# Set-up of a recurrent attention kernel: first score product in quarters between weight products, paired transposes, and dummy matmuls in idle gaps

## Chip, core and metric

The kernel runs on one core of one Trainium2 chip. The metric is device time in microseconds (us). The kernel before had a median of 1601.96 us in its first three timed runs.

## The reference, cut to what matters

```python
def _A_ref(x, mem0, Wq, Wk, Wv, Wo, seg_len):        # 64 segments of 32 rows, 8 memory rows
    for s in range(n_seg):                            # strictly one after the other
        h = concatenate([mem, xs], axis=1)            # 40 rows x 448
        q, k, v = h @ Wq, h @ Wk, h @ Wv              # 16 heads of 256
        p = softmax(where(mask, q @ k.T * scale, -1e9))
        o = (p @ v) @ Wo
        mem = o[:, :8]                                # feeds the next segment
def _B_ref(x, W_gate, W_up, W_down): ...              # gated feed-forward, 448 -> 1792 -> 448
x = x + A(layernorm(x)); x = x + B(layernorm(x)); x = x + A(layernorm(x)); x = x + B(layernorm(x))
```

The kernel multiplies the weights together first. For each head, M = Wk Wq^T gives scores as h M h^T, and B = Wv Wo gives outputs as p (h B). These products are the set-up. Then 70 steps follow, one segment of each of two layers at a time.

## The kernel before

The set-up loads Wk and Wq transposed by DMA (`load_kq`), and Wv and Wo plain (`load_vo`). `make_M(i)` makes M for four heads, and `make_B(j)` makes B for two heads, after transposing Wv on TensorE.

```python
def make_B(j):
    wn, wo = vo.pop(j)
    wv = bp.tile([P, 4, DM], BF, tag="wv", name="wv")
    for a in range(2):                       # 16 transposes through PSUM
        ...
        copy_out(wv[:, 2 * a:2 * a + 2, :], tp[:, :, 0:DM])
    for hh in range(2):
        for mt in range(3):                  # 16 matmuls of 448 columns, with the tails
            ...
    ...
load_vo(0); load_vo(1); load_kq(0)
make_B(0); load_vo(2); make_B(1); load_vo(3); load_kq(1); make_M(0)
...                                          # mem0, layernorm of the first two x tiles
for j in (2, 3): make_B(j); load_vo(j + 2)
load_kq(2); make_M(1); load_kq(3)
for j in (4, 5): make_B(j); load_vo(j + 2)
in_order(nc.sync.dma_start(x_ring[:, 2:R, :], ...))
make_M(2); make_M(3)
for g in range(nsteps):
    ...
    if g == 0:
        def mid(): make_B(6)                 # between the first G and the scores
        def soft(): make_B(7); late_pools()  # after the softmax was started
    ...
    step(g, inG, mid, soft, before, late, end, last)
    ...
fill(1, 20)                                  # the last feed-forward
```

Each step begins with G = M h, 224 matmuls with 40 or 80 moving columns into PSUM (`gps`). Scores (`S_ps`), softmax, values (`vps`), the transposes of P (`PT_ps`), the weighted sum (`AT_ps`) and the new memory (`mps`) follow. `tails` are the products of the last 64 of the 448 rows. They read `MT_sb`, and the full ones read `M_sb`.

```python
        def tail(self, i):
            t, half = self.t0 + i, HALVES[self.side]
            self.mm(t, MT_sb[half, t * 128:(t + 1) * 128], hT[half, 3, c0:c1, :])
        ...
        first = [pair_of_banks(k) for k in range(nA)]
        tails(first)
        for pr in first:
            for bk in pr:
                bk.full()
                bk.out()
```

In the profiles PE is TensorE, DVE VectorE, ACT ScalarE, POOL GpSimd and SP SyncE, whose queue issues the loads. In the timelines below its pieces of work run in the order of the program: while it waits in front of one (1.28 us for wq before M3), nothing from behind it runs.

## Time and profile before

| | kernel before |
|---|---|
| three timed runs | 1601.85 to 1602.24 us |
| the profiled execution | 1604.42 us (its span 1602.6) |
| M3 starts | 56.12 us |
| first G starts | 61.63 us |
| G of step 1 starts | 90.62 us |
| last matmul of M3 (61.35) to G of step 1 | 29.27 us |

The profiled execution was 2.5 us longer than the median of the timed runs.

The page of the kernel before, its line of busy times and its chain of work that ended last:

```profile
PE 1564.1 (98%) x38808; PEld 1177.5 (73%) x38808; DVE 941.8 (59%) x2154; ACT 659.4 (41%) x1502; POOL 143.0 (9%) x370
...
PE 92%; DVE 4%; SPq 2%; DMA 2%; ACT 1%; issue 0%; POOL 0%; POOLq 0%; ACTq 0%
```

TensorE bounds the kernel: PE is busy for 98% of the span and makes up 92% of the chain. For this change the question is only where PE stands still, and for that the timeline is the right view.

The timeline of PE in the kernel before, from M3 to G of step 1. Columns are start, duration, line, operation, shape and count. The bracket gives the idle time before, and what ended it.

```profile
56.12 5.58 PE L126 MATMUL ps<-wq,wk 128*128 128x448 bf16 x32 [1.28 <-DMA wq<-in_A_Wq_dram]
61.63 0.57 PE L126 MATMUL gps<-hTr,MT_sb 64*128 64x40 bf16 x32
62.13 2.99 PE L126 MATMUL gps<-hTr,M_sb 128*128 128x40 bf16 x112
66.60 2.00 PE L126 MATMUL gps<-hTr,M_sb 128*128 128x40 bf16 x56 [1.48 <-issue]
...
71.36 2.95 PE L126 MATMUL ps<-wo,wv 128*128 128x448 bf16 x16 [0.61 <-ACT wv L187]
...
77.72 2.95 PE L126 MATMUL ps<-wo,wv 128*128 128x448 bf16 x16 [1.23 <-DVE wv L189]
...
81.96 0.36 PE L126 MATMUL vps<-BT_sb,memTp 64*32 64x448 bf16 x2 [0.80 <-DVE BT_sb L189]
...
90.62 0.57 PE L126 MATMUL gps<-hTr,MT_sb 64*128 64x40 bf16 x32 [0.28 <-DVE hTr L631]
```

Read it as a list of holes: 1.28 for the load of wq, 1.48 that no semaphore explains ("issue"), 0.61 and 1.23 for copies of transposed Wv, 0.80 for a copy of B. In the second half of the first G the matmuls also run slower: 56 take 2.00 us, while 112 took 2.99 us before. The table by stretches shows a granted clock of 0.50 there. Its columns are the stretch, its length, the busy time of PE, PEld (weight loads), DVE, ACT and POOL, then PEclk, the granted clock (1.00 is full), the DMA share and GB/s:

```profile
66.00:68.00 2.00, 1.40 (x43) 1.40 (x43) 0.00 (x0) 0.00 (x0) 0.00 (x0) 0.68 0.03 8
68.00:70.00 2.00, 2.00 (x52) 1.67 (x49) 0.66 (x1) 0.56 (x1) 0.00 (x0) 0.50 0.00 0
```

The sync queue issues loads without a break from 0.7 to 58 us. These are its last four transposed issues, with start and duration:

```profile
34.79 7.04 SPq L165 DMA_TRANSPOSE wk<-in_A_Wk_dram  x1
41.88 4.51 SPq L165 DMA_TRANSPOSE wq<-in_A_Wq_dram  x1
46.49 3.46 SPq L165 DMA_TRANSPOSE wk<-in_A_Wk_dram  x1
50.00 3.88 SPq L165 DMA_TRANSPOSE wq<-in_A_Wq_dram  x1
```

### The profile page before, as it was taken

How to read it: one execution, taken by the hardware profiler on the slowest of the kernel's cores; microseconds unless marked ns; L12 is line 12 of the kernel's file. 1: busy time of each engine (PE TensorE's matmuls, PEld its weight loads, DVE VectorE, ACT ScalarE, POOL GpSimd, SP SyncE). 2: the span in 40 equal slices, each digit the busy share in tenths (PEclk: the TensorE clock that was granted, in tenths of full speed). 3: DMA queues.
4: the chain of work that ended last, by engine and by line, in shares of the span. 5: the costliest groups of instructions: out<-in, count | busy, mean ns of one | idle time of the engine just before them, and what ended most of it. 6: DMA issues, size and time to landing. Idle time of an engine off the chain costs nothing.

```text
span 1602.6 us, 82607 instructions
## 1 busy us (share of the span) xinstructions
PE 1564.1 (98%) x38808; PEld 1177.5 (73%) x38808; DVE 941.8 (59%) x2154; ACT 659.4 (41%) x1502; POOL 143.0 (9%) x370
## 2 busy tenths in 40 slices
PE   7889999999999999999999999999999999999998
PEld 4467677777777777877778777877778777877675
DVE  6545556656656566656655566556655556556554
ACT  5533344434444344434444344434344343434333
POOL 2000001000101001000100101000100101000000
PEclk9999999999999999999999999999999999999999
DMA  9631000000000000000000000000000000000000
GB/s 238 148 96 34 5 6 4 6 11 6 5 10 6 11 6 10 6 11 6 5 11 6 11 6 10 6 11 6 5 11 6 8 5 6 6 8 6 7 5 9
DMA packets 49541, 31.22 MB, mean 19 GB/s; under 512 B 31656, under 2 KB 48304, under 8 KB 49200
## 3 DMA queue, kind: packets, MB, share of 16 engines
q1 hardware_dynamic: 49168, 25.93, 6.5%
q8 instruction: 303, 4.96, 1.2%
q14 instruction: 38, 0.31, 0.1%
q10 hardware_dynamic: 32, 0.01, 0.0%
HBM read 14.00 MB, written 1.84 MB: 10 GB/s over the span
## 4 chain that ended last, share of the span: by engine, by line
PE 92%; DVE 4%; SPq 2%; DMA 2%; ACT 1%; issue 0%; POOL 0%; POOLq 0%; ACTq 0%
PE gps L126 30%; PE vps L126 28%; PE gate L126 11%; PE AT_ps L126 7%; PE S_ps L126 6%; PE dps L126 5%; PE PT_ps L129 2%; DMA wq<-in_A_Wq_dram 2%; SPq L165 1%; PE tps L129 1%; DVE vox L382 1%; PE up L126 1%; PE ps L126 1%; PE mps L126 1%; DVE ssum L534 0%
## 5 line engine op out<-in xcount | busy, mean ns | idle before, releaser
L126 PE MATMUL gps<-hTr,M_sb 128*128 128x80 bf16 (+1 forms) x11760 | 417.7, 198 | 1.6 <-issue 1.5
L126 PEld LDWEIGHTS <-M_sb 128*128 128x128 bf16 x11760 | 406.2, 99 | 5.9 <-issue 1.8
L460 DVE CAST G<-gps 128x480 bf16<-128x480 f32 (+3 forms) x326 | 193.9, 612 | 237.3 <-PE gps L126 237.1
L126 PEld LDWEIGHTS <-hTr 128*32 128x32 bf16 (+3 forms) x7936 | 197.0, 96 | 145.2 <-issue 38.7
L460 ACT CAST G<-gps 128x480 bf16<-128x480 f32 (+3 forms) x326 | 165.7, 527 | 325.2 <-PE gps L126 325.2
L126 PE MATMUL vps<-B_sb,hTr 128*32 128x448 bf16 x4608 | 241.9, 353 | 0.0
L126 PE MATMUL gate<-xnT,Wgu 64*128 64x128 bf16 x3136 | 202.7, 216 | 1.0 <-ACT xnT L305 1.0
L126 PE MATMUL up<-xnT,Wgu 64*128 64x128 bf16 x3136 | 203.2, 216 | 0.0
L126 PEld LDWEIGHTS <-Wgu 64*128 64x128 bf16 x6272 | 181.4, 94 | 19.2 <-issue 12.4
L382 ACT CAST VOm<-vps 128x448 bf16<-128x448 f32 x245 | 118.9, 529 | 144.8 <-PE vps L126 144.6
L126 PE MATMUL vps<-B_sb,memTp 128*32 128x448 bf16 x3360 | 171.7, 353 | 0.0
L382 ACT CAST vox<-vps 128x448 bf16<-128x448 f32 x192 | 99.4, 533 | 159.3 <-PE vps L126 159.3
L126 PEld LDWEIGHTS <-memTp 128*32 128x32 bf16 (+1 forms) x4480 | 98.5, 94 | 82.1 <-issue 3.7
L382 DVE CAST vox<-vps 128x448 bf16<-128x448 f32 x192 | 116.5, 619 | 58.9 <-PE vps L126 58.8
L318 DVE SCALAR_TENSOR_TENSOR hh<-gate,ut 128x256 bf16<-128x256 f32 x224 | 94.7, 423 | 66.3 <-ACT ut L317 66.2
L126 PEld LDWEIGHTS <-PT 128*64 128x64 bf16 x2048 | 96.4, 110 | 39.4 <-issue 18.9
L317 ACT CAST ut<-up 128x256 bf16<-128x256 f32 x224 | 83.8, 374 | 63.1 <-PE up L126 61.9
L126 PE MATMUL AT_ps<-VOm,PT 128*64 128x320 bf16 (+1 forms) x1280 | 97.7, 261 | 1.2 <-DVE PT L576 1.2
L528 DVE TENSOR_REDUCE mx<-S_ps 104x8 f32<-104x320 f32 (+1 forms) x140 | 62.2, 486 | 59.2 <-PE S_ps L126 59.2
L126 PE MATMUL gps<-hTr,MT_sb 64*128 64x80 bf16 (+1 forms) x3920 | 91.3, 195 | 2.7 <-ACT hTr L631 1.6
L126 PE MATMUL dps<-Wd,hh 128*128 128x448 bf16 x448 | 92.6, 353 | 0.0
L126 PE MATMUL S_ps<-G,hTr 128*40 128x160 bf16 (+1 forms) x1792 | 88.1, 245 | 0.7
(89 smaller groups left out, 1428.0 us busy)
## 6 DMA issues: line engine op xcount, KB each, us to landing
wo<-in_A_Wo_dram SPq DMA_DIRECT2D x8, 448.0 KB, 5.3
wvn<-in_A_Wv_dram SPq DMA_DIRECT2D x8, 384.0 KB, 3.7
y<-mb SPq DMA_DIRECT2D x96, 28.0 KB, 1.8
out_dram<-x_ring SPq DMA_DIRECT2D x16, 112.0 KB, 1.7
Wgu<-in_B_W_gate_dram SPq DMA_DIRECT2D x7, 224.0 KB, 3.3
Wgu<-in_B_W_up_dram SPq DMA_DIRECT2D x7, 224.0 KB, 3.5
Wd<-in_B_W_down_dram SPq DMA_DIRECT2D x7, 224.0 KB, 3.3
x_ring<-in_A_x_dram SPq DMA_DIRECT2D x10, 112.0 KB, 2.0
```

Source lines behind the costliest of these rows:

```text
L126: in_order(nc.tensor.matmul(*a, **k))
L129: in_order(nc.tensor.transpose(*a))
L165: in_order(nc.sync.dma_start_transpose(t[:], srcs[n][:, 1024 * i:1024 * (i + 1)]))
L317: recent["ut"] = nc.scalar.copy(ut[:], gu[1][:])
L318: recent["hh"] = nc.vector.scalar_tensor_tensor(out=self.hh[:, f:f + 2, :], in0=gu[0][:], scalar=0.0, in1=ut[:], op0=ALU.max, op1=ALU.mult)
L382: op = self.evac[2 * x + e](self.dst[:, 2 * e + x, :], self.ps[x][e][:, 0:DM])
L460: op = (cp_a, cp_v)[self.side](G[:, self.side, self.t0:self.t0 + self.n, c0:c1, :], self.ps[:, 0:self.n * NP].rearrange("p (m c t) -> p m ...
L528: nc.vector.tensor_reduce(mx[RR, e], S3, axis=AX.X, op=ALU.max)
```

## The change

The intent is to move PE work out of the serial stretch after the last load into the waits for loads, to hide copies behind other work, and to keep PE busy in short idle gaps. The diff, cut to its core (the class `Bank` only moves, and `GPhase.run` is the old code):

```diff
+    def turn_B(j):                      # the transposes, taken out of make_B
...
+        def quarter(self, k):
+            pr = self.pair((7, 7, 7, 7), k)
+            self.tails(pr)
+            for bk in pr:
+                bk.full()
+                bk.out()
...
+    def make_two(j):
+        turn_B(j)
+        turn_B(j + 1)
+        for i in (j, j + 1):
+            make_B(i)
+            load_vo(i + 2)
+
+    def warm(n):
+        ps = psum.tile([P, 512], F32, tag="ps", name="warm")
+        for _ in range(n):
+            matmul(ps[:, 0:DM], ident[:], M_sb[:, 0, 0:DM], start=True, stop=True)
...
+    first_G.append(GPhase(0))
+    first_G[0].quarter(0)
     make_M(1)
     load_kq(3)
-    for j in (4, 5):
-        make_B(j)
-        load_vo(j + 2)
+    make_two(4)
...
+    first_G[0].quarter(1)
     make_M(2)
+    first_G[0].quarter(2)
     make_M(3)
+    turn_B(6)
+    turn_B(7)
+    first_G[0].quarter(3)
...
             def mid():
                 make_B(6)
+                make_B(7)
             def soft():
-                make_B(7)
                 late_pools()
...
+        if g in (1, 3):
+            def before():
+                warm(5)
...
+    warm(10)
     fill(1, 20)
```

More of the change, by code (lines that the diff above doesn't have):

```diff
@@ L215, in make_M @@
             store_M(MT_sb[:, 896 * i:896 * i + 896], e, ps[:, 0:DM])
-    def make_B(j):
-        wn, wo = vo.pop(j)
-        wv = bp.tile([P, 4, DM], BF, tag="wv", name="wv")
+    wv_T = {}
+    def turn_B(j):
+        wn = vo[j][0]
+        wv = wv_T[j] = bp.tile([P, 4, DM], BF, tag="wv", name="wv")
         for a in range(2):
@@ L227, in make_B @@
             copy_out(wv[:, 2 * a:2 * a + 2, :], tp[:, :, 0:DM])
+    def make_B(j):
+        wv, wo = wv_T.pop(j), vo.pop(j)[1]
         for hh in range(2):
@@ L420, in build_kernel, with __init__, mm, full @@
     cp_v = nc.vector.tensor_copy
+    class Bank:
+        def __init__(self, gp, side, t0, n):
+            self.gp, self.side, self.t0, self.n = gp, side, t0, n
+            self.ps = psum.tile([P, 512], F32, tag="ps", name="gps")
+            self.fresh = True
+        def mm(self, t, w, rhs):
+            o = (t - self.t0) * self.gp.NP
+            matmul(self.ps[:, o:o + self.gp.NP], w, rhs, start=self.fresh, stop=False, skip_group_check=True)
+            self.fresh = False
+        def full(self):
+            gp = self.gp
+            for t in range(self.t0, self.t0 + self.n):
+                m = 7 * (2 * (t // 7) + self.side) + t % 7
+                for kd in range(3):
+                    self.mm(t, M_sb[:, kd, m * 128:(m + 1) * 128], gp.hT[:, kd, gp.c0:gp.c1, :])
+        def tail(self, i):
+            gp = self.gp
+            t, half = self.t0 + i, HALVES[self.side]
+            self.mm(t, MT_sb[half, t * 128:(t + 1) * 128], gp.hT[half, 3, gp.c0:gp.c1, :])
+        def out(self):
+            gp = self.gp
+            op = (cp_a, cp_v)[self.side](
+                gp.G[:, self.side, self.t0:self.t0 + self.n, gp.c0:gp.c1, :],
+                self.ps[:, 0:self.n * gp.NP].rearrange("p (m c t) -> p m c t", m=self.n, t=L))
+            if self.side:
+                load_when(op)
+                recent["G"] = op
+                if not self.t0:
+                    recent["G1"] = op
@@ new lines, in build_kernel, with __init__, pair, tails @@
+    class GPhase:
+        def __init__(self, g):
+            chains = [c for c in (C1, C2) if 0 <= g - c.lag < nseg]
+            self.both = len(chains) == 2
+            self.c0, self.c1 = chains[0].cid, chains[-1].cid + 1
+            self.NP = L * (self.c1 - self.c0)
+            self.hT = hTr[:, g % NR]
+            self.G = p_vo.tile([P, 2, NGH, 2, L], BF, tag="G", name="G")
+        def pair(self, banks, k):
+            return [Bank(self, side, sum(banks[:k]), banks[k]) for side in range(2)]
+        @staticmethod
+        def tails(pr):
+            for i in range(pr[0].n):
+                for bk in pr:
+                    bk.tail(i)
+        def quarter(self, k):
+            pr = self.pair((7, 7, 7, 7), k)
+            self.tails(pr)
+            for bk in pr:
+                bk.full()
+                bk.out()
+        def run(self, inG):
+            banks = (6, 6, 6, 6, 4) if self.both else (7, 9, 12)
+            nA = 3 if self.both else 2
+            first = [self.pair(banks, k) for k in range(nA)]
+            for pr in first:
+                self.tails(pr)
+            for pr in first:
+                for bk in pr:
+                    bk.full()
+                    bk.out()
+            inG()
+            then = [self.pair(banks, k) for k in range(nA, len(banks))]
+            for pr in then:
+                for bk in pr:
+                    bk.full()
+            for pr in then:
+                self.tails(pr)
+                for bk in pr:
+                    bk.out()
@@ L422, in step @@
+    first_G = []
     def step(g, inG, mid, soft, before, late, end, last):
@@ L431, in step @@
         hT = hTr[:, rg]
-        G = p_vo.tile([P, 2, NGH, 2, L], BF, tag="G", name="G")
-        banks = (6, 6, 6, 6, 4) if both else (7, 9, 12)
-        class Bank:
-            def __init__(self, side, t0, n):
-                self.side, self.t0, self.n = side, t0, n
-                self.ps = psum.tile([P, 512], F32, tag="ps", name="gps")
-                self.fresh = True
-            def mm(self, t, w, rhs):
-                o = (t - self.t0) * NP
-                matmul(self.ps[:, o:o + NP], w, rhs, start=self.fresh, stop=False, skip_group_check=True)
-                self.fresh = False
-            def full(self):
-                for t in range(self.t0, self.t0 + self.n):
-                    m = 7 * (2 * (t // 7) + self.side) + t % 7
-                    for kd in range(3):
-                        self.mm(t, M_sb[:, kd, m * 128:(m + 1) * 128], hT[:, kd, c0:c1, :])
-            def tail(self, i):
-                t, half = self.t0 + i, HALVES[self.side]
-                self.mm(t, MT_sb[half, t * 128:(t + 1) * 128], hT[half, 3, c0:c1, :])
-            def out(self):
-                op = (cp_a, cp_v)[self.side](
-                    G[:, self.side, self.t0:self.t0 + self.n, c0:c1, :],
-                    self.ps[:, 0:self.n * NP].rearrange("p (m c t) -> p m c t", m=self.n, t=L))
-                if self.side:
-                    load_when(op)
-                    recent["G"] = op
-                    if not self.t0:
-                        recent["G1"] = op
@@ L469, in pair_of_banks @@
-        def pair_of_banks(k):
-            t0 = sum(banks[:k])
-            return [Bank(side, t0, banks[k]) for side in range(2)]
-        def tails(pairs):
-            for pr in pairs:
-                for i in range(pr[0].n):
-                    for bk in pr:
-                        bk.tail(i)
-        nA = 3 if both else 2
-        first = [pair_of_banks(k) for k in range(nA)]
-        tails(first)
-        for pr in first:
-            for bk in pr:
-                bk.full()
-                bk.out()
@@ L486, in step @@
-        inG()
-        then = [pair_of_banks(k) for k in range(nA, len(banks))]
-        for pr in then:
-            for bk in pr:
-                bk.full()
-        for pr in then:
-            tails([pr])
-            for bk in pr:
-                bk.out()
+        gp = first_G[0] if g == 0 else GPhase(g)
+        if g:
+            gp.run(inG)
+        G = gp.G
         S_ps = [psum.tile([P, 512], F32, tag="ps", name="S_ps") for _ in HALVES]
@@ L673, in build_kernel @@
     load_kq(0)
-    make_B(0)
-    load_vo(2)
-    make_B(1)
-    load_vo(3)
+    make_two(0)
     load_kq(1)
@@ L686, in build_kernel @@
         prep_pe(C1, t)
-    for j in (2, 3):
-        make_B(j)
-        load_vo(j + 2)
+    make_two(2)
     load_kq(2)
+    first_G.append(GPhase(0))
+    first_G[0].quarter(0)
     make_M(1)
     load_kq(3)
-    for j in (4, 5):
-        make_B(j)
-        load_vo(j + 2)
+    make_two(4)
     if R > 2:
         in_order(nc.sync.dma_start(x_ring[:, 2:R, :], x_dram[256:R * 128].rearrange("(t p) d -> p t d", p=P)))
+    first_G[0].quarter(1)
     make_M(2)
+    first_G[0].quarter(2)
     make_M(3)
+    turn_B(6)
+    turn_B(7)
+    first_G[0].quarter(3)
     nc.gpsimd.tensor_copy(memTp[0][:, :, 0:16], hTr[:, 1, :, 0, 0:16])
```

## The prediction

> **What bounds the kernel.** TensorE: on the page PE is busy 98% of the span and the chain that ended last is 92% PE. From 240 to 1440 us the table by stretches shows PE 99.3 to 99.8% busy at granted clock 1.00. The change touches none of that: in instruction order only set-up, step 0 and three places for dummy matmuls differ, and the DMA order is identical. Only the first 90 us and the last 15 can move.
>
> **Set-up (0 to 62 us).** The sync queue issues without a break from 0.7 to 58 us and DMA is saturated (share 1.03 to 1.16 from 10 to 60 us). The weight products M0 to M3 each wait for their transposed wq: idle 0.33, 0.88, 1.59, 1.28 us, starting at 17.45, 33.31, 49.26, 56.12. Those arrivals stay. PE also waits 0.3 to 1.2 us per weight transpose for its copy-out (wv, 3.9 us in all).
> **After the last load (61.6 to 90.6 us).** Everything is serial on PE: the whole first G (61.63 to 69.3), with a 1.48 us stall called "issue" and the clock at 0.50 until about 70; two make_B with their transposes (to 80.6; waits 0.61 and 1.23), softmax entangled with their copies, 0.8 us wait for BT_sb, P transposes at 86.28, step 1's G at 90.62.
> [...]
>
> **What the change does.**
> 1. G(0) becomes four quarters, three of them moved between M products, into DMA waits. A quarter is about 1.33 us (5.33 us for the same work in step 1). Off the tail: 4 us, the stall (1.5) and most of the half-clock loss (about 1.5).
> 2. Transposes are paired, so copy-outs hide: 0.61+1.23 us in step 0, and set-up slack that absorbs quarters 0 and 1.
> 3. make_B(6), (7) both precede softmax: the waits for BT_sb and Px vanish.
> Cost: quarter 2 sits directly behind M2 and needs M2's last MT_sb copy, which ended 0.85 us after M2 (55.69 against 54.84). So M3 starts about 57.0: +0.9.
> Estimated schedule: M3 ends 62.6; transposes to 64.75; quarter 3 to 66.1; mask 66.35; B6, B7 to 72.1; scores 73.3; values and P transposes at 77.9 instead of 86.28. Gain 8.4 us.
> 4. warm(5) in steps 1 and 3: 448-column matmuls at 0.189 us each, 0.94 us inside an idle of 1.12: 0 to +0.1. The clock was already 1.00.
> 5. warm(10) before the last feed-forward: 1.89 us into an idle of 1.15, at clock 1.00: the tps transposes move from 1589.20 to 1589.77: +0.57.
>
> Net -7.8 us: predicted **1594.3 us**, range 1592.6 to 1597.0. Chances: faster by over 2% 0.005; within 2% 0.985; slower 0.01.
>
> **What would show it.** Right: M0 to M2 start within 0.5 us of before; M3 near 57.0, behind quarter 2 and its copy; no "issue" stall and clock 1.00 from 62 to 72; no wait for wv in step 0; P transposes of step 0 near 78, step 1's G near 82.2; steady part as long as before; tps about 0.6 later relative to the last score step. Wrong: M3 still at 56.1; a stall or half clock elsewhere.
>
> **What would make it wrong.** [...] half clock returning in step 0 (+2); the last wvn landing after 63; quarter 2 waiting less (-0.9); warm(5) delaying the P transposes; the clock in the last feed-forward being lower in unprofiled runs, so that warm(10) gains.

-8.4 us up to the P transposes of step 0 and +0.57 for `warm(10)` come to the -7.8. The 0.189 us of a 448-column matmul is in the trace: in `dps` of the kernel before (1585.23 us) the matmuls start 0.189 to 0.199 us apart.

## The result, and the profile after

| | before | after |
|---|---|---|
| median of timed runs, these rounds | 1602.46 us (12 runs, 1600.36 to 1604.98) | 1596.06 us (10 runs, 1594.58 to 1598.37) |
| ratio, 95% interval | | 0.996 (0.9951 to 0.997) |
| M3 starts | 56.12 us | 57.10 us |
| G of step 1 starts | 90.62 us | 83.65 us |
| last matmul of M3 to G of step 1 | 29.27 us | 19.66 us |

Ratios here and below are the mean time of one kernel's fast runs over that of the other's in the same rounds, so they are not quite the ratio of the medians quoted.

The page of the changed kernel, the same two lines:

```profile
PE 1567.5 (98%) x38828; PEld 1179.3 (74%) x38828; DVE 941.9 (59%) x2155; ACT 659.2 (41%) x1503; POOL 142.9 (9%) x370
...
PE 93%; DVE 3%; DMA 2%; SPq 1%; ACT 0%; issue 0%; POOL 0%; ACTq 0%
```

The timeline of PE in the changed kernel, from M2 to G of step 1:

```profile
48.48 5.58 PE L126 MATMUL ps<-wq,wk 128*128 128x448 bf16 x32 [0.34 <-DMA wq<-in_A_Wq_dram]
54.32 0.24 PE L126 MATMUL gps<-hTr,MT_sb 64*128 64x40 bf16 x6 [0.26 <-ACT MT_sb L187]
54.97 0.27 PE L126 MATMUL gps<-hTr,MT_sb 64*128 64x40 bf16 x8 [0.41 <-ACT MT_sb L187]
55.17 1.22 PE L126 MATMUL gps<-hTr,M_sb 128*128 128x40 bf16 x42
57.10 7.25 PE L126 MATMUL ps<-wq,wk 128*128 128x448 bf16 x32 [0.70 <-DMA wq<-in_A_Wq_dram]
64.28 1.96 PE L129 MATMUL tp<-ident,wvn 128*128 128x128 bf16 x32
66.17 0.34 PE L126 MATMUL gps<-hTr,MT_sb 64*128 64x40 bf16 x14
66.45 1.23 PE L126 MATMUL gps<-hTr,M_sb 128*128 128x40 bf16 x42
...
67.85 5.83 PE L126 MATMUL ps<-wo,wv 128*128 128x448 bf16 x32
...
83.65 0.57 PE L126 MATMUL gps<-hTr,MT_sb 64*128 64x40 bf16 x32 [0.28 <-DVE hTr L664]
```

From the end of M3 to the scores no hole is left: the waits of 1.48, 0.61, 1.23 and 0.80 us are gone. Two things are new. M3 takes 7.25 us where it took 5.58, and it starts 0.98 us later, again after a wait for wq. The table by stretches shows the half clock again, now inside M3:

```profile
57.00:58.00 1.00, 0.90 (x3) 0.40 (x3) 0.00 (x0) 0.00 (x0) 0.00 (x0) 0.55 0.90 263
58.00:59.00 1.00, 1.00 (x5) 0.38 (x3) 0.62 (x1) 0.21 (x1) 0.00 (x0) 0.50 0.83 125
```

The last four transposed issues of the changed kernel:

```profile
34.96 7.49 SPq L165 DMA_TRANSPOSE wk<-in_A_Wk_dram  x1
42.49 3.59 SPq L165 DMA_TRANSPOSE wq<-in_A_Wq_dram  x1
46.18 4.86 SPq L165 DMA_TRANSPOSE wk<-in_A_Wk_dram  x1
51.09 3.85 SPq L165 DMA_TRANSPOSE wq<-in_A_Wq_dram  x1
```

The first of the four is long in both. Of the other three, now the third of the list is long, where the second was.

At the end of the span, the kernel before and then the changed kernel: the last half of a feed-forward (`dps`), and the first transposes of the last one (`tps`):

```profile
1585.23 2.82 PE L126 MATMUL dps<-Wd,hh 128*128 128x448 bf16 x14
1589.20 0.56 PE L129 MATMUL tps<-ident,xd 128*128 128x128 bf16 x7 [1.15 <-DVE xd L263]
```

```profile
1578.45 2.82 PE L126 MATMUL dps<-Wd,hh 128*128 128x448 bf16 x14
1581.11 2.06 PE L126 MATMUL warm<-M_sb,ident 128*128 128x448 bf16 x10
1583.00 0.55 PE L129 MATMUL tps<-ident,xd 128*128 128x128 bf16 x7
```

From the start of `dps` to `tps` is 3.97 us before and 4.55 us after. The ten dummies do not fit their gap and cost 0.58 us.

### The profile page after: what moved, and what is told of

Its sections match the earlier page's. It is cut to its first block, busy times and chain, and to the rows that moved or that the text cites. A ratio compares the mean times of both kernels' runs of the same rounds, so it can differ in the third digit from the quotient of the medians.

```text
span 1596.4 us, 82645 instructions
## 1 busy us (share of the span) xinstructions
PE 1567.5 (98%) x38828; PEld 1179.3 (74%) x38828; DVE 941.9 (59%) x2155; ACT 659.2 (41%) x1503; POOL 142.9 (9%) x370
## 3 DMA queue, kind: packets, MB, share of 16 engines
q8 instruction: 303, 4.96, 1.2%
## 4 chain that ended last, share of the span: by engine, by line
PE 93%; DVE 3%; DMA 2%; SPq 1%; ACT 0%; issue 0%; POOL 0%; ACTq 0%
PE gps L126 30%; PE vps L126 28%; PE gate L126 11%; PE AT_ps L126 7%; PE S_ps L126 6%; PE dps L126 6%; PE PT_ps L129 2%; PE ps L126 2%; PE tps L129 1%; DVE vox L388 1%; DMA wq<-in_A_Wq_dram 1%; SPq L165 1%; PE up L126 1%; PE mps L126 1%; DMA wvn<-in_A_Wv_dram 0%
## 5 line engine op out<-in xcount | busy, mean ns | idle before, releaser
L455 DVE CAST G<-gps 128x480 bf16<-128x480 f32 (+2 forms) x327 | 193.9, 610 | 232.9 <-PE gps L126 232.5
L455 ACT CAST G<-gps 128x480 bf16<-128x480 f32 (+2 forms) x327 | 165.8, 525 | 321.8 <-PE gps L126 321.8
```

The costliest lines, as they stand in the source:

```text
L455: op = (cp_a, cp_v)[self.side](gp.G[:, self.side, self.t0:self.t0 + self.n, gp.c0:gp.c1, :], self.ps[:, 0:self.n * gp.NP].rearrange("p (m ...
```

## The experiments

Twelve runs were made, three of them of an unmodified kernel, and all gave correct results. Timed intervals are about 2 us wide either way, so most verdicts rest on one profile of each kernel. These measures are used:

- the *tail*: from the start of the last matmul of M3 to the start of G of step 1;
- a *half-clock window*: a record of granted clock 0.5. Every such window inside a kernel, once the clock was full, lasted 3.413 us;
- the listed clock of each execution: 1.000, 0.999, 0.998 and 0.997 are read as 0, 1, 2 and 3 such windows (one window is 3.413/2 of 1600 us, so 0.1%). In all fourteen profiles this agrees with the windows counted inside the kernel.

### 1. Two more looks at the changed kernel

No edit. The control ran once with the second batch (`after_again`) and once with the last (`after_third`).

> The changed kernel unmodified, as the control of this batch and for a second profile. In the ten runs so far seven had a mean clock of 1.000 and three 0.999, and the three were about 2.2 us longer. Theory: the half-clock window that the first profile shows inside M3 (57.1 to 60.5 us) comes and goes between executions, so runs fall in two groups about 2 us apart that the listed clock separates; a profile that catches none has M3 at 5.6 us instead of 7.25 and step 1's G start 8.4 to 8.7 us before that of the kernel before (90.62). Rival: the half clock is there always and the groups are something else; then M3 takes 7.25 us in this profile too.

> The changed kernel unmodified, as control on the same chip as the repaired one. Expected: 5 to 7 us below the kernel before; last tps about 0.58 us later after step 69's start than in profiles without the ten dummies; M3 7.7 to 8.7 us after M2.

| | time, median | ratio to before | M3 start | M3 to the transposes behind it | tail |
|---|---|---|---|---|---|
| first profile | 1596.06 | 0.996 | 57.10 | 7.18 | 19.66 |
| after_again | 1596.78 | 0.9968 (0.9954 to 0.9982) | 56.59 | 5.52 | 19.69 |
| after_third | 1598.70 | 0.9965 (0.9952 to 0.9978) | 57.74 | 7.09 | 19.66 |

The tail is the same to 0.03 us. The half-clock window inside M3 comes and goes: it was there in the first and third profile (57.1 and 57.6 us), and not in the second, where M3 took 5.58 us:

```profile
56.59 5.58 PE L126 MATMUL ps<-wq,wk 128*128 128x448 bf16 x32
```

So a part of the spread between executions is the clock, as expected. It is not all of it: in `after_again` the two executions with a window were 4 us longer than the three without, and not 2.2. Two expected sizes were missed: in `after_again` G of step 1 started 9.1 us before that of the kernel before (8.4 to 8.7 expected), and in `after_third` M3 started 9.06 us after M2 (7.7 to 8.7 expected).

### 2. The kernel before

> The kernel before, unmodified, for a second profile. Theory [...]: the stall inside the first G of step 0 is there again, 0.5 to 2 us, and the third 16 KiB instruction packet of the span starts [...]after 62 us. Rival (an accident of one execution): no idle over 0.3 us inside the first G. The number and place of half-clock windows may differ from the first profile (66.7 us).

Its single time was 1606.06 us. There was no stall at all in the first G: 168 full products in one row, and a tail of 26.60 us where the first profile had 29.27. This contradicts the expectation that the stall is always there. The timeline of PE:

```profile
63.14 0.57 PE L126 MATMUL gps<-hTr,MT_sb 64*128 64x40 bf16 x32
63.64 4.40 PE L126 MATMUL gps<-hTr,M_sb 128*128 128x40 bf16 x168
```

The records tie the stall to an instruction packet that starts late. The DMA records of the trace give the start of each 16 KiB packet of the instruction queue (q8: 303 packets, 4.96 MB), and the instruction records give how many PE instructions, weight loads included, had started by then:

| profile with a whole first G behind M3 | third packet starts | PE instructions started by then | stall |
|---|---|---|---|
| before | 64.20 us | 901 | 1.48 us, after instruction 961 |
| before_warm5 (below) | 65.33 us | 839 | 0.55 us, after instruction 961 |
| before_again | 64.07 us | 771 | none |
| before_x_late (below) | 62.01 us | 771 | none |

Both stalls stand behind the same instruction, and they end 2.40 and 2.25 us after the packet's start. In the two profiles without a stall, the next instruction started 2.40 and 2.43 us after the packet. So in all four it started 2.25 to 2.43 us after the packet did, and PE stood still where the packet was late. That PE waits there for the packet is the reading of these four profiles. The packet's start differs between executions (62.01 to 65.33 us). The rival, that the burst of small matmuls stalls by itself, is out: the burst is the same in all four. The cause supposed, that full DMA engines hold the packet back, was a guess and is not shown: from 63 to 64 us, just before the packet's start, the DMA share was 0.23 in the kernel before, with the stall, and 1.02 in `before_again`, without one.

### 3. The kernel before with the large x load moved away

```diff
-    in_order(nc.sync.dma_start(x_ring[:, 2:R, :], ...))
...
             def mid():
+                loads.append((x_ring[:, 2:R, :], ...))   # issued at the softmax of step 0
                 make_B(6)
```

> The kernel before with the 448 KB load of x tiles 2 to 5 issued at the softmax of step 0 instead of at 57.5 us, so that the DMA queues are empty some 1.5 us earlier. Nothing in PE's order changes. Theory [...]: the stall in the first G shrinks to under 0.7 us, and step 1's G starts 1 to 3 us earlier. Rival (the stall comes from the burst of 144 pairs of small instructions itself): it stays at about 1.5 us.

No stall, a tail of 26.61 us, and the third packet at 62.01 us. The time did not fall: 1604.09 us, ratio 1.0003 (0.999 to 1.0015). The profile had a half-clock window in step 1 (99.3 us), which cost 1.37 us there. Since `before_again` had no stall either, one profile cannot show that the move removed it. The third packet did start earlier than in the other three (64.07 to 65.33 us), but that the load delays it is not shown.

### 4. Each main part of the change alone

`only_quarters` keeps the four quarters, and undoes the pairing, the order and the dummies. `no_quarters` keeps the pairing and the order. Both edits are shortened, and comments stand for the rest:

```diff
 # only_quarters
     def make_two(j):
-        turn_B(j)
-        turn_B(j + 1)
         for i in (j, j + 1):
+            turn_B(i)
             make_B(i)
...
 # make_B(7) and its transposes back in soft(), no warm(5), no warm(10)

 # no_quarters
-        gp = first_G[0] if g == 0 else GPhase(g)
-        if g:
-            gp.run(inG)
+        gp = GPhase(g)
+        gp.run(inG)         # the whole G at the start of step 0, after turn_B(6), turn_B(7)
 # the four calls of quarter() and first_G.append() taken out
 # no warm(5), no warm(10)
```

> Of the change only step 1: G(0) in four quarters; transposes not paired, make_B(7) back behind the score matmuls, no dummy matmuls. If the quarters carry most of the gain as the forecast had it (4 us of G, 1.5 of stall, 1.5 of half clock, less 0.9), the time is 4.5 to 6.5 us below the kernel before, and 2 to 3.5 us above the changed kernel. If pairing and order carry most, it is less than 3 us below the kernel before. No stall of the kind called issue is expected in step 0[...].

> Of the change only the paired transposes and both make_B before the softmax; the first G is whole, in step 0, after the transposes of tiles 6 and 7; no dummy matmuls. Forecast's accounting: 3.8 to 5.3 us below the kernel before, and about 3 us above the changed kernel. [...]

| | ratio to before | tail | gain in the tail against the undisturbed 26.60 |
|---|---|---|---|
| quarters alone | 0.9987 (0.9975 to 1.0) | 23.73 | 2.87 us |
| pairing and order alone | 0.9979 (0.9967 to 0.9991) | 23.47 | 3.13 us |
| the whole change | 0.996, 0.9968, 0.9965 | 19.66 to 19.69 | 6.9 us |

The quarters gained about 2.1 us in time (0.13% of 1602; 0 to 4.0 by the interval), and not the expected 4.5 to 6.5; their median lay 5.1 us above the changed kernel, where 2 to 3.5 were expected. That accounting took a stall of 1.5 us and a half clock as given. Of three profiles of this order one had both, one a stall of 0.55 us alone, and one neither. Pairing and order gained 3.4 us (1.4 to 5.3), a little below what was expected (3.8 to 5.3), but not clear of it. In `no_quarters` the equally long first G ran without a stall (the third packet started at the 712th instruction), which says no more than `before_again` does.

The two parts together gain 0.9 us more in the tail than separately. The timeline of `only_quarters` shows why: without the transposes in between, quarter 3 stands directly behind M3 and waits for its copy, which the paired transposes hide in the whole change.

```profile
57.87 5.58 PE L126 MATMUL ps<-wq,wk 128*128 128x448 bf16 x32
63.92 0.64 PE L126 MATMUL gps<-hTr,MT_sb 64*128 64x40 bf16 x14 [0.47 <-DVE MT_sb L189]
```

### 5. The dummies in steps 1 and 3

`no_warm5` is the changed kernel without them, and `before_warm5` is the kernel before with them.

```diff
 # no_warm5
-        if g in (1, 3):
-            def before():
-                warm(5)
 # before_warm5: the same three lines added to the kernel before
```

> The changed kernel without the five dummy matmuls in steps 1 and 3. Theory (idle filler): no change in time, steps 1 and 3 both 14.69 us as before. Rival (they guard the clock): some executions get a half-clock window in step 1 or 3, with a listed clock of 0.999 or 0.998 and about 1.7 us more, so the mean rises by 0.3 to 1.7 us.

> The kernel before with only the five dummy matmuls in steps 1 and 3. Theory (idle of 1.65 us in one 3.4 us window lets the clock fall in step 1 or 3 in some executions, and each such window costs 1.4 us there): the listed clock loses fewer windows than the kernel before, whose nine runs of the last batch lost 1.6 windows on average (1.000, 0.999, 0.998, 0.997 read as 0, 1, 2, 3), and the time falls by 0.5 to 1.5 us. Rival, which the forecast held (clock there is full anyway): no change in clock or time.

The timeline of PE in `no_warm5`, step 1. The row with `AT_ps` takes 3.20 us, where the same row takes 1.72 us in the changed kernel:

```profile
92.48 0.27 PE L129 MATMUL PT_ps<-ident,Px 40*128 40x40 bf16 x4 [1.12 <-DVE Px L575]
92.95 0.27 PE L129 MATMUL PT_ps<-ident,Pm 40*128 40x40 bf16 x4 [0.20 <-DVE Pm L575]
93.55 3.20 PE L126 MATMUL AT_ps<-VOm,PT 128*64 128x320 bf16 x16 [0.33 <-DVE PT L609]
```

The table by stretches of `no_warm5` puts the half clock there:

```profile
92.00:94.00 2.00, 0.98 (x10) 0.68 (x11) 1.13 (x3) 0.71 (x2) 0.00 (x0) 0.87 0.73 229
94.00:96.00 2.00, 2.00 (x13) 1.53 (x11) 0.00 (x0) 0.00 (x0) 0.00 (x0) 0.50 0.80 202
```

Step 1 took 16.07 us in it, and 14.69 in the changed kernel, so the window cost 1.38 us. Over all fourteen profiles: of the seven without these dummies, five had a half-clock window in step 1 (`before_again` had another in step 3). Of the seven with them, none had one in either step.

The traces also show when these windows come. In each profile all half-clock windows start on one grid of 3.413 us (in `before_again` 50.99, 102.19 and 132.91 us are 15 and 9 grid steps apart), and the place of this grid differs between executions (the windows at 66.71 us in the kernel before and at 57.10 us in the changed kernel are 2.8 steps apart). From 17.5 us on, all fourteen windows inside the kernels begin at the end of a grid cell in which PE stood idle for 1.37 to 2.69 us, summed over its gaps. That much is not always enough: nine other cells with 1.43 to 1.79 us of idle were followed by full clock. The 1.65 us of idle in step 1 lay in one cell in all five profiles with a window there. In the other two the grid cut it, with at most 1.13 us (the kernel before) and 1.32 us (`no_quarters`) in a cell. The dummies take away 1.12 of these 1.65 us.

Where the dummies stood they cost nothing measurable: steps 1 and 3 are within 0.02 us of the undisturbed length in the first profile of the changed kernel.

The timed runs do not resolve this. `no_warm5` has ratio 0.9958 (0.9946 to 0.9971), which is not above its control's 0.9968. `before_warm5` has 1.0001 (0.9988 to 1.0014), and its listed clocks (five windows in six executions) were no better than those of the kernel before in that batch (ten in eleven). Its profile had its only window in the last feed-forward instead, as the table by stretches shows:

```profile
1592.00:1594.00 2.00, 2.00 (x50) 2.00 (x46) 0.42 (x1) 0.37 (x1) 0.00 (x0) 0.58 0.02 4
```

From `tps` to the end took 15.04 us there, and 13.4 in every other profile.

### 6. The dummies before the last feed-forward

```diff
-    warm(10)
     fill(1, 20)
```

> The changed kernel without the ten dummy matmuls before the last feed-forward. Theory (cost only): the last tps transposes start 0.6 us sooner after the last dps, the clock at the end stays 1.00, the time falls by 0.6 us against the unmodified changed kernel. Rival (they guard the clock): without them some executions have a half-clock window in the last feed-forward, and the time rises by up to 1.7 us in those, on average by 0 to 1 us.

In its profile the 0.58 us were gone and the clock at the end was full. The time was 1597.09 us, ratio 0.9962 (0.9949 to 0.9974), which cannot be told from the control. So the cost is shown on the profile alone. What the dummies are meant against was seen as well: among eight profiles without dummies at the end, one (`before_warm5`, above) had a half clock in the last feed-forward, for 1.64 us. None of the six with dummies did. With so few, one in eight is only a rough share. At that share the ten dummies cost more (0.58 us) than they save (about 0.2, an estimate: 1.64 us in one of eight).

### 7. Instruction packets and the transposed loads

In the changed kernel the quarters bring PE instructions forward, and from 46 to 62 us two 16 KiB instruction packets start where the kernel before has none. The DMA view for 46 to 62 us, first of the kernel before and then of the changed kernel, with packets, MB and share of the 16 engines (q8 is the queue of the 16 KiB packets):

```profile
q1 hardware_dynamic: 11570, 4.32, 107.5%
```

```profile
q1 hardware_dynamic: 10706, 3.80, 107.2%
q8 instruction: 2, 0.03, 0.8%
```

The trace's DMA records give their starts: 43.13 us in the kernel before, 48.82 and 57.54 us in the changed kernel. The first of each falls into the transposed issue that was long in the two lists above. To test it, tiny dummies were put into PE's waits in the kernel before:

```diff
+    pad(30)          # 8-column matmuls, in the wait for wq in front of M1
     make_M(1)
...
+    pad(60)          # in front of M2
     make_M(2)
     make_M(3)
```

> The kernel before with 30 tiny dummy matmuls (8 columns) put in front of M1 and 60 in front of M2, inside PE's waits for wq (0.8 and 1.6 to 2.3 us idle). They change no load and little PE time, but bring the third 16 KiB instruction packet forward from about 64 us to about 49 to 52 us. Theory (an instruction packet falling into a transposed load holds that load up by about 1 us): one of the last two transposed issues (wk3, wq3) takes 4.4 to 5.3 us instead of 3.4 to 4.0, and M3 starts 7.8 to 8.7 us after M2 instead of the 6.9 of three profiles of the kernel before; the stall in the first G is gone. Rival (in the changed kernel quarter 2 behind M2, or its memory traffic, delays M3 and the load): both stay at 3.4 to 4.0 and 6.9 us.

The third packet came at 51.34 us. The long issue moved with it, from the second to the last of the four, as the sync queue's timeline of `before_pad` shows:

```profile
42.27 3.91 SPq L165 DMA_TRANSPOSE wq<-in_A_Wq_dram  x1
46.28 3.45 SPq L165 DMA_TRANSPOSE wk<-in_A_Wk_dram  x1
49.77 4.70 SPq L165 DMA_TRANSPOSE wq<-in_A_Wq_dram  x1
```

M3 then waited 2.00 us for wq and started 7.58 us after M2. Three profiles of the kernel before or its variants had 6.85 to 6.93 (`before_again`, with M2 at half clock, had 7.20). So a shift of about 0.7 us came, less than expected (to 7.8 to 8.7). Over all fourteen profiles, the last three transposed issues took 4.36 to 5.30 us where a packet started inside them (14 issues), and 3.36 to 3.99 us where none did (28 issues). So the one of these three issues that a packet falls into is longer, by about 1 us (an estimate from these ranges). In the issue before these three, the first of the lists above, this is not seen: 5.90 to 7.77 us without a packet inside (nine profiles), 7.33 to 8.03 with one (five). Nor does it follow that the total is longer. In the kernel before the packet hits M2's load, and in the changed kernel one of M3's. M3 starts between 55.57 and 58.02 us in five profiles of the kernel before and its lightly edited forms, and between 56.59 and 57.74 in three of the changed kernel. Whether the extra packet delays M3 overall cannot be told within this spread, and it stays open. The time was unchanged, ratio 1.0004 (0.999 to 1.0018); a window in step 1 again cost 1.3 us in the profile.

### 8. What limits M3 in the changed kernel

```diff
     make_M(2)
-    first_G[0].quarter(2)
     make_M(3)
     turn_B(6)
     turn_B(7)
+    first_G[0].quarter(2)
     first_G[0].quarter(3)
```

> The changed kernel with quarter 2 moved from between M2 and M3 to just ahead of quarter 3. Theory (M3 is limited by the arrival of wq3, held up by the instruction packet, at 7.8 to 8.7 us after M2's start): M3 starts no more than 0.5 us earlier relative to M2 and now waits 1.5 to 2.5 us for wq; quarter 2's 1.3 us come back behind M3; step 1's G starts 1.0 to 1.5 us later. Rival (quarter 2 and its wait for MT_sb limit M3, as forecast): M3 starts 0.9 to 1.5 us earlier and step 1's G within 0.5 us of the changed kernel.

M2 happened to wait 2.07 us in this profile and ran at half clock, so that M3 came 7.2 us after M2's start with no wait, and the interesting wait could not appear. M3's start (57.73) was 6.17 us after the issue of its wq. Where M3 waited for that load, with the packet in the issue before it, it started 5.9 to 6.1 us after the issue (four profiles). The trace also tells when the load landed: 5.95 us after its issue, so at 57.51, 0.22 us before M3 started. So M3 could have started at most about 0.2 us sooner, which supports the limit by the load. In the three profiles of the changed kernel M3 started 0.04 to 0.06 us after that landing, `after_again` included, where no wait is recorded. The tail was 21.09 us, 1.4 more than the changed kernel, as expected for quarter 2's work coming back. The time was 1600.73 us, ratio 0.998 (0.9968 to 0.9993).

### 9. Two repairs

```diff
         def quarter(self, k):
             pr = self.pair((7, 7, 7, 7), k)
+            if k == 2:                  # full products first: MT_sb is copied meanwhile
+                for bk in pr:
+                    bk.full()
+                self.tails(pr)
+                for bk in pr:
+                    bk.out()
+                return
...
-    warm(10)
+    warm(5)
     fill(1, 20)
```

> Two repairs of the changed kernel: quarter 2 does its full products first and its tails last, so that it need not wait for M2's MT_sb copy; and the dummy matmuls before the last feed-forward are five, not ten, so that they fit in the 1.15 us of idle. Expected: the two waits of 0.26 and 0.41 us behind M2 gone; last tps 0.57 us sooner after the last dps; time 0.6 to 1.2 us below the changed kernel (the first part gains nothing where wq3 arrives late). If it is not faster by 0.3 us or more in the profile from step 69 to the end, the cost of the ten dummies is wrong.

Both repairs did what was meant locally: no wait for `MT_sb`, and 3.97 us from `dps` to `tps`, with the five dummies in between. The timeline of PE shows what became of the first:

```profile
55.37 1.22 PE L126 MATMUL gps<-hTr,M_sb 128*128 128x40 bf16 x42
56.52 0.34 PE L126 MATMUL gps<-hTr,MT_sb 64*128 64x40 bf16 x14
58.34 7.26 PE L126 MATMUL ps<-wq,wk 128*128 128x448 bf16 x32 [1.47 <-DMA wq<-in_A_Wq_dram]
```

The time freed went into one longer wait for wq, and M3 ran at half clock. The median was 1598.8 us, ratio 0.9964 (0.9952 to 0.9975), while the unmodified changed kernel on the same chip had 0.9965. So there is no gain overall. The two executions with a full clock took spans of 1594.5 and 1593.7 us, against 1595.4 to 1596.7 for the four of the control. But four of the six had a window, against one of five. The pattern of section 5 fits: the 1.47 us lay in one grid cell here, and so did 1.37 and 1.62 us in the first and third profile of the changed kernel, while `after_again` and `no_warm10` had at most 0.76 us in a cell there, and no window. That the single long wait makes the window likelier is still a guess from few counts. A version that fills this wait with dummies was not run.

## Why the prediction was right or wrong

The result, 1596.06 us, lies inside the range (1592.6 to 1597.0), and "within 2%" was right. The centre, 1594.3, was 1.8 us too low. That it was no further off is partly luck: two terms that the forecast did not have, about -1 us from the dummies in steps 1 and 3 and +1.1 us from a half clock in M3, nearly cancel (below).

**Right, with sizes.**

- *The schedule of the tail.* The forecast had M3 ending at 62.6 and step 1's G at 82.2, which is 19.6 us. Measured from the transposes behind M3 to that G: 19.37, 19.41 and 19.38 in three profiles of the changed kernel. The waits for wv, BT_sb and Px in step 0 are gone, and no stall appeared from 62 us on.
- *warm(10).* Forecast +0.57 us, measured +0.58.
- *warm(5) fits its gap.* Forecast cost 0 to +0.1, measured 0.
- *M3's start, in number.* Forecast 57.0; it started at 57.10, 56.59 and 57.74. The reason given was wrong (below), so this is luck too. M2 started 0.78 us earlier than before in the first profile, outside the 0.5 us that the forecast allowed.

**Wrong in size.**

- *Point 1: "the stall (1.5) and most of the half-clock loss (about 1.5)".* This was counted as a sure saving of 3.0 us. The first profile of the kernel before did lose 2.67 us there (a tail of 29.27, against 26.60 undisturbed). But `before_again` lost 0, and `before_warm5`, whose order is the same up to that point, lost 0.71. The mean of the three is 1.1 us, so the term was about 1.9 us too large. The mistake was to read the losses off one execution that took 1604.42 us and to subtract them from a median of 1601.96 us of other executions, which need not contain them.
- *The half clock does return.* The forecast named this as a risk (+2 in step 0). It came inside M3 instead, in two of three profiles, for 1.6 to 1.7 us each. The forecast's "set-up slack that absorbs" the quarters did not consider that waits left between pieces of small matmuls (0.26, 0.41 and 0.70 us in the first profile) can be followed by half clock in the next product.
- *Point 4: "The clock was already 1.00."* So it was in the one profile read, in which the window had fallen into the first G. Five of seven profiles without the dummies had a window in step 1, which cost 1.3 to 1.4 us in four of them and 0.6 in the fifth, and one had another in step 3, for 1.1 us. The dummies are worth about 1 us on average by the profiles (an estimate: these losses, 7.1 us in all, over seven profiles), though the timed runs don't resolve it. The forecast gave this part nothing.

Together: the tail undisturbed -6.9; stall and half clock in the first G -1.1; steps 1 and 3 about -1; half clock in M3 +1.1 (1.66, 0 and 1.57 in three profiles); warm(10) +0.58. That is -7.3, without the change in M3's start, which is about +0.4 (the mean of three profiles against that of five) and not resolved. The timed ratios say -5.1 to -6.4. So a remainder of 1 to 2 us, of the size of the intervals, is not accounted for.

**Wrong in reason.** *"M3 starts about 57.0: +0.9"*, because quarter 2 waits for M2's last copy. That wait is there (0.26 + 0.41 us). But in the first and third profile M3 afterwards still waited 0.70 and 1.15 us for wq, and taking the copy wait away (`mended`) only lengthened that. The arrival of wq limits M3 in those executions: M3 started within 0.06 us of it. In `after_again` M3 followed quarter 2 without a wait, but wq had landed only 0.06 us before, so there too an earlier quarter 2 would have gained next to nothing. The forecast also held the loads to be untouched, since their order was. Their order was, but the instruction packets shifted among them (43.13 us before, 48.82 and 57.54 us after).

## What to carry to other kernels

Before subtracting a loss seen in one profile, ask whether that execution is the typical one: compare its time with the timed runs, and look at a second profile. A stall or a half-clock window that comes and goes is worth its mean, not its size. When work is moved into a wait, fill what is left of it with dummies that fit: in step 1 none of seven profiles with them had a half-clock window, and five of seven without them had one. Look at the sum of the idle pieces too: here 1.37 us, in three pieces within one 3.413 us grid cell, was once followed by half clock for 3.413 us, though nine cells with 1.43 to 1.79 us were not. Whether pieces fall into one cell differed between executions, so such a loss is a chance and not a constant. And moving instructions can also move the instruction packets among the loads: here a transposed issue with a packet inside took 4.36 to 5.30 us, and one without 3.36 to 3.99 us.
